# Gated mix of a complex state-space recurrence and a long convolution: convolution by a 32 x 64 transform in 64-row tiles with x kept in SBUF, recurrence over 8 time phases in stacks of 64 states, output in three column parts

## The chip, the cores and the metric

The kernel runs on one core of a Trainium2 chip. A core has a matrix engine (TensorE; PE in the profile, with its weight loads shown apart as PEld), a vector engine (DVE), a scalar engine (ACT), a general engine (POOL) and a queue engine (SP). TensorE reads from the on-chip memory SBUF (128 partitions) and writes to the accumulators in PSUM (8 banks of 512 fp32 words per partition); the other engines carry results from PSUM back to SBUF. DMA moves data between device memory and SBUF. The metric is the device time of one execution in microseconds; lower is better.

## The reference, cut to what matters

S = 2048 time steps, D = 1024 channels, P = 1024 complex states, all inputs in bf16. `_A_ref` is a linear recurrence with complex states, `_B_ref` a causal convolution of length 2048 per channel, and a gate mixes the two.

```python
def _A_ref(x, Lambda_re, Lambda_im, B_re, B_im, C_re, C_im, log_dt, Dskip):
    ...
    Lam_bar = jnp.exp(dt * Lam)
    B_bar = ((Lam_bar - 1.0) / Lam)[:, None] * Bmat
    Bu = jnp.einsum("bld,pd->blp", x + 0j, B_bar)
    ...
    for t in range(L):
        h = Lam_bar[None, :] * h + Bu[:, t, :]
        hs.append(h)
    ...
    y = 2.0 * jnp.einsum("blp,dp->bld", hseq, Cmat).real + x * Dskip[None, None, :]

def _B_ref(q, k, v, shift_k, ssm_k, ssm_D):
    ...
    for t in range(ks):
        k_shift = k_shift + k_pad[:, t:t + S, :] * shift_k[:, ks - 1 - t][None, None, :]
    kv = k_shift * v
    ...
    y = y + kv * ssm_D[None, None, :]
    return q * y

x = A_x
g = _sigmoid((x * gate_w).sum(-1, keepdims=True))
a = _A_ref(x, A_Lambda_re, A_Lambda_im, A_B_re, A_B_im, A_C_re, A_C_im, A_log_dt, A_Dskip)
b = _B_ref(x, B_k, B_v, B_shift_k, B_ssm_k, B_ssm_D)
return g * a + (1 - g) * b
```

Between the two lines on kv, `_B_ref` computes the causal convolution of kv with ssm_k by transforms of twice the length.

## The kernel before, in words

The work is written as a list of operations (`op`, and `dma` for transfers), each with an engine, a planned duration, the tiles it reads and writes, and a due time (the tables `PS`, `PU`, `PO`, `PC`, `PH`, `PG`). A planner, `_Plan.schedule`, runs through them in planned time, gives each a place in one of 21 slabs of SBUF or in PSUM, and so fixes the order on every engine; some operations may go to a second engine (`alt`), as evacuations from PSUM do (`evac`, line 520: ACT, or else DVE). `emit` then writes the instructions in that order. At run time an engine takes its instructions in order and waits by semaphores.

Recurrence (`s5`). x arrives by transposing DMA as four tiles `xT`, even and odd times in two halves of 512. For each of 8 groups of 128 states, `gemm_u` (line 882) multiplies x by the group's B, real and imaginary part apart, 512 columns a time; for even times the previous odd time's part comes in through the small diagonal matrices `dg` (lines 889, 892). `rot` turns the even times by a table of angles, scans them over time with a real factor (line 923) and turns them back (line 911 and the adds behind it); `odd` (lines 948, 950) makes the odd times from the even ones. Four of the 8 groups go to device memory (`h_scr`) and are read again for the output.

Convolution (`conv`), in 8 units of 128 channels. `kvprep` makes kv (lines 724 to 739) with channels on partitions and writes it to `kv_scr`; `load_A` reads it, and ssm_k, with 8 channels times 16 time blocks on partitions. `stage1` (line 747) takes the transform of length 16, `spec` (lines 760 to 762) the one of length 128, `product` (lines 772, 776) multiplies the two spectra on DVE, `inverse` (lines 786 to 788) goes back by the length 128, a DMA from slab to slab brings the 16 blocks onto partitions (line 515, four for each quarter), and `final` (lines 805 to 808) ends the transform, multiplies by x, read once more, and writes the result to `pB_scr`.

Output (`outp`). For each of 2 halves of the columns and 16 blocks of 128 rows, 16 matmuls of 512 columns (line 1125) sum h times C over the states; x (line 1099, times Dskip) and the convolution's result (line 1107, times 1 - g) come from device memory and are added (lines 1113, 1134). C is loaded by transposing DMA and scaled on ACT and DVE (lines 1053 to 1065).

At the start, 24 small matmuls (line 397) and the function `keep` (lines 1002 to 1014, several tile shapes) fill the time before x arrives; `gates` (line 964) computes the gate with weights of 32 columns.

The matmul of the transform in `gemm_u` reads

```python
PE_.matmul(ps.ap[:, ri, k0:k1], lhsT=BT.ap[:, d, ri, :], rhs=t.ap[:, d, k0:k1],
```

and that of the first step of the convolution, in `stage1`,

```python
PE_.matmul(ps.ap[:, i, :], lhsT=a.ap[:, 8 * q + i, :], rhs=t1v[:, hh * 128:(hh + 1) * 128],
```

## Time and profile before

| what | before |
|---|---|
| median of 3 runs | 431.93 us (429.65 to 432.07) |
| span of the profiled execution, first to last instruction | 427.0 us |
| median less span | 4.9 us |
| TensorE busy, granted clock | 398.4 us, 0.990 |
| VectorE, ScalarE, GpSimd busy | 346.7, 267.8, 132.7 us |
| DMA | 71.87 MB, 168 GB/s over the span |
| instructions | 7194, of them 2691 matmuls |

The profile is one execution. Busy time is the time in which an engine has an instruction running; matmuls are pipelined, so a matmul's mean duration is longer than its distance from the next, and the busy time of a dense run of matmuls counts each moment once. A group's line gives the source line, the engine, the operation, out<-in, shapes and count, then busy time, mean ns of one, and the idle time just before them with what ended it. For a matmul, 128*64 is the size of the stationary operand: rows (the contraction) by columns; 128x256 is the moving operand.

### The profile page before, as it was taken

To read this page: it belongs to the slowest core of one execution; us is meant where nothing else is said; L and a number is where in the kernel's file an instruction comes from. 1 tells how busy PE (TensorE), PEld (TensorE's weight loads), DVE (VectorE), ACT (ScalarE), POOL (GpSimd) and SP (SyncE) were. 2 spreads that over 40 slices of the span, in tenths; PEclk is the share of its full clock that TensorE was granted. 3 is DMA by queue.
4 is the path that set the end of the run, shared out by engine and by line. 5 is a ranking of instruction groups with operands and counts; after the bars stand their busy time and mean duration, and the time that the engine had idled before them with its cause. 6 is when DMAs were issued, how large, how long until landed. Compare 5 with 4: busy or idle time off the path is not lost.

```text
span 427.0 us, 7194 instructions
## 1 busy us (share of the span) xinstructions
PE 398.4 (93%) x2691; PEld 228.5 (54%) x2736; DVE 346.7 (81%) x513; ACT 267.8 (63%) x310; POOL 132.7 (31%) x172
## 2 busy tenths in 40 slices
PE   7598999999999789999969999899989999999996
PEld 6353544655566456566635655676544444444442
DVE  4998999999979789989889989979696969724422
ACT  3489488747589679477966786999554286203100
POOL 6994611232464134753634403340010000000000
PEclk9999999999999999999998999999999999999999
DMA  8999999459999999598999369999989996405111
GB/s 149 113 196 195 194 232 231 174 90 160 158 186 193 256 217 185 127 207 173 187 184 164 90 192 166 287 184 178 174 163 185 213 234 205 143 22 177 49 37 62
DMA packets 153596, 71.87 MB, mean 168 GB/s; under 512 B 129861, under 2 KB 147541, under 8 KB 153561
## 3 DMA queue, kind: packets, MB, share of 16 engines
q1 hardware_dynamic: 146120, 54.55, 69.8%
q0 software_dynamic: 7360, 16.85, 16.9%
q8 instruction: 21, 0.34, 0.4%
q14 instruction: 15, 0.11, 0.1%
q10 hardware_dynamic: 80, 0.01, 0.0%
HBM read 24.93 MB, written 16.79 MB: 98 GB/s over the span
## 4 chain that ended last, share of the span: by engine, by line
PE 68%; DMA 11%; SPq 10%; ACT 4%; DVE 3%; issue 3%; POOL 0%; DVEq 0%; ACTq 0%; POOLq 0%
PE ps L1125 22%; PE ps L882 20%; SPq L513 8%; DMA slab<-slab 5%; PE ps L760 4%; ACT slab L520 4%; PE ps L747 4%; DMA slab<-in_A_x_dram 4%; PE ps L889 3%; PE ps L950 3%; DMA slab<-in_B_ssm_k_dram 3%; PE ps L761 2%; PE ps L786 2%; PE ps L762 2%; SPq L515 2%
## 5 line engine op out<-in xcount | busy, mean ns | idle before, releaser
L520 ACT CAST slab<-ps 128x1024 bf16<-128x1024 f32 x197 | 185.4, 1042 | 62.8 <-PE ps L892 17.6
L882 PE MATMUL ps<-slab,slab 128*128 128x512 bf16 (+1 forms) x527 | 115.8, 370 | 6.3 <-DMA slab<-in_A_B_re_dram 3.1
L1125 PE MATMUL ps<-slab,slab 128*128 128x512 bf16 x485 | 109.1, 379 | 1.0 <-DVE slab L1134 0.4
L882 PEld LDWEIGHTS <-slab 128*128 128x128 bf16 x544 | 52.8, 99 | 60.0 <-issue 5.5
L1125 PEld LDWEIGHTS <-slab 128*128 128x128 bf16 x512 | 49.8, 98 | 59.6 <-issue 0.7
L515 POOL DMA_DIRECT2D slab<-slab x84 | 51.4, 618 | 57.8 <-ACT slab L520 51.9
L1134 DVE SCALAR_TENSOR_TENSOR slab<-ps,gcols,slab 128x512 bf16<-128x512 f32 x32 | 23.6, 747 | 39.1 <-PE ps L1125 36.1
L1107 ACT ACTIVATE slab<-slab,omgc 128x512 bf16<-128x512 bf16 x32 | 21.2, 714 | 45.2 <-DMA slab<-pB_scr 40.1
L760 PE MATMUL ps<-slab,fC 128*128 128x512 bf16 x118 | 44.9, 381 | 1.1 <-ACT slab L520 0.6
L747 PE MATMUL ps<-tab,slab 128*128 128x128 bf16 x512 | 35.0, 222 | 7.5 <-POOL slab L712 6.2
L911 DVE TENSOR_TENSOR slab<-slab,slab 128x2048 bf16<-128x2048 bf16 x31 | 37.7, 1217 | 3.5 <-PE ps L747 1.5
L772 DVE TENSOR_TENSOR slab<-slab 128x2048 bf16<-128x2048 bf16 x32 | 38.6, 1215 | 1.8 <-ACT slab L520 1.5
L747 PEld LDWEIGHTS <-slab 128*128 128x128 bf16 x512 | 31.4, 99 | 12.3 <-POOL slab L712 6.8
L761 PE MATMUL ps<-slab,fS 128*128 128x256 bf16 x128 | 35.0, 273 | 0.6 <-issue 0.2
L762 PE MATMUL ps<-slab,fN 128*128 128x256 bf16 x128 | 35.0, 274 | 0.0
L786 PE MATMUL ps<-slab,gC 128*128 128x256 bf16 x128 | 29.9, 273 | 1.7 <-DVE slab L776 1.7
L776 DVE TENSOR_TENSOR slab<-slab 128x512 bf16<-128x512 bf16 x64 | 24.9, 416 | 6.3 <-PE ps L950 2.3
L788 PE MATMUL ps<-slab,gS 128*128 128x128 bf16 x128 | 28.0, 219 | 0.0
L787 PE MATMUL ps<-slab,gN 128*128 128x128 bf16 x128 | 28.0, 219 | 0.0
L735 DVE TENSOR_TENSOR slab<-slab,slab 128x2047 bf16<-128x2047 bf16 (+2 forms) x22 | 26.7, 1213 | 0.0
L808 DVE TENSOR_TENSOR slab<-ps,slab 128x1024 bf16<-128x1024 f32 x16 | 19.3, 1216 | 3.3 <-PE ps L806 2.8
L1113 DVE SCALAR_TENSOR_TENSOR slab<-slab,gcols,slab 128x512 bf16<-128x512 bf16 x26 | 18.3, 745 | 3.5 <-ACT slab L1107 3.4
(184 smaller groups left out, 532.5 us busy)
## 6 DMA issues: line engine op xcount, KB each, us to landing
slab<-in_A_x_dram SPq DMA_DIRECT2D x22, 256.0 KB
slab<-slab POOLq DMA_DIRECT2D x84, 64.0 KB, 5.3
slab<-h_scr SPq DMA_DIRECT2D x8, 512.0 KB
slab<-pB_scr SPq DMA_DIRECT2D x16, 256.0 KB
out_dram<-slab SPq DMA_DIRECT2D x15, 256.0 KB
slab<-in_B_ssm_k_dram SPq DMA_DIRECT2D x7, 512.0 KB
pB_scr<-slab SPq DMA_DIRECT2D x12, 256.0 KB
slab<-slab SPq DMA_DIRECT2D x44, 64.0 KB
```

Of the source, the lines that this page charges most:

```text
L513: nc.sync.dma_start_transpose(out=o_, in_=i_)
L515: QS[q].dma_start(out=o_, in_=i_)
L520: op("ACT", 1.04, lambda: A.copy(o_(), i_()), r=r, w=w, prio=prio, alt=("DVE", 1.2, lambda: V.tensor_copy(o_(), i_())))
L747: PE_.matmul(ps.ap[:, i, :], lhsT=a.ap[:, 8 * q + i, :], rhs=t1v[:, hh * 128:(hh + 1) * 128], start=True, stop=True)
L760: PE_.matmul(ps.ap[:, i], lhsT=fC[:, k2, :], rhs=zz, start=True, stop=False)
L761: PE_.matmul(ps.ap[:, i, :, 0, :], lhsT=fS[:, k2, :], rhs=zz[:, :, 1, :], start=False, stop=False)
L762: PE_.matmul(ps.ap[:, i, :, 1, :], lhsT=fN[:, k2, :], rhs=zz[:, :, 0, :], start=False, stop=True)
L772: TT(out=T.ap, in0=K.unsqueeze(2).to_broadcast([128, 2, 2, 4 * CH]), in1=W_.unsqueeze(1).to_broadcast([128, 2, 2, 4 * CH]), op=ALU.mult)
L786: PE_.matmul(ps.ap[:, i], lhsT=gC[:, k2, :], rhs=pp.ap[:, :, i, :], start=True, stop=False)
L882: PE_.matmul(ps.ap[:, ri, k0:k1], lhsT=BT.ap[:, d, ri, :], rhs=t.ap[:, d, k0:k1], start=(d == 0), stop=(par == 1 and d == ND - 1))
L911: TT(out=out, in0=tab.ap.unsqueeze(2).to_broadcast([128, 2, 2, CW]), in1=x.unsqueeze(1).to_broadcast([128, 2, 2, CW]), op=ALU.mult)
L1125: PE_.matmul(ps.ap, lhsT=Hr[pi, a // 4].ap[:, par, ri, (a % 4) * 128:(a % 4 + 1) * 128], rhs=CT[pi, dh][0].ap[:, CT[pi, dh][1], ri, :], st ...
```

## The change

The kernel is rewritten around the same planner (places are now in units of 1 KB of 9 slabs, due times in one table). What it does now:

- x stays in SBUF in natural layout as `X` (16 row groups of 128, 32 KB a partition); it is scaled by 1 - g there, multiplied by the convolution's result there, and added in the output. `pB_scr` and `kv_scr` are gone.
- The transform of the convolution is 32 times 64. `stage1` uses the data as the stationary operand, in four tiles of 64x64, and so has time on partitions at once; `spec` uses two tiles of 128x64; `inverse` two of 64x128, with two or four terms (`TERMS`: for four, the sums of the complex product are left to PSUM, and `product` leaves out its two adds). Where DMA brought blocks onto partitions, DVE transposes blocks of 32x32 (`turn` in `kvprep`, `flip`).
- The recurrence has 64 states, real and imaginary part stacked, on 128 partitions. Time is cut in 8 phases (t mod 8) of 256. `gemm` adds up four phases in a chain, in two halves (`hn`, `jn`), the scan runs over 256 (`turned`), and `fill` makes the other phases from it.
- All of h goes to device memory except that the last two groups are used from SBUF in part one. The output runs in three column parts (`PARTS`: 256, 512, 256 columns); each part reads h again, part three only the half that part two's tiles don't still hold (`SHARE`). The output's matmuls use two tiles of 128x64, and x times Dskip is a matmul for all rows.
- C isn't scaled any more (the factor is in the recurrence's small matrices); three DMAs swap halves of each C tile.

Core of the diff (removed lines only where they stand for a replaced function):

```diff
-    NSLAB, NPS = 21, 8
+    NSLAB, NPS = 9, 8
...
+TERMS = (2,2,2,4,4,4,4,4)
...
+PARTS = ((0,2),(2,4),(6,2))
+SHARE = {(2, ph): (1, ph) for ph in range(4, 8)}
...
+    X = consts.tile([128, 16, D], BF16, name="X")
...
-        def stage1(a, z, w, hh, q, pr):
+        def stage1(a, z, w, j, pr):
...
-                for i in range(8):
-                    PE_.matmul(ps.ap[:, i, :], lhsT=a.ap[:, 8 * q + i, :], rhs=t1v[:, hh * 128:(hh + 1) * 128],
-                               start=True, stop=True)
+                for i in range(8):
+                    for h in range(2):
+                        for r_ in range(2):
+                            PE_.matmul(ps.ap[64 * r_:64 * r_ + 64, h, i, :], lhsT=av_[64 * h:64 * h + 64, 8 * j + i, :],
+                                       rhs=t1[64 * h:64 * h + 64, r_].rearrange("p k b -> p (k b)"), start=True, stop=True)
+            evac(lambda: z.ap[:, :, w, :].rearrange("p k (h b c) -> p k h b c", h=2, b=2)[:, :, :, :, 8 * j:8 * j + 8],
+                 lambda: ps.ap.rearrange("p h c (k b) -> p k h b c", b=2), r=[ps], w=[(z, (w, j))], pr=pr)
...
-        def spec(z, kv, q, h, pr):
+        def spec(z, kv, q, hh, pr):
...
-                    PE_.matmul(ps.ap[:, i], lhsT=fC[:, k2, :], rhs=zz, start=True, stop=False)
-                    PE_.matmul(ps.ap[:, i, :, 0, :], lhsT=fS[:, k2, :], rhs=zz[:, :, 1, :], start=False, stop=False)
-                    PE_.matmul(ps.ap[:, i, :, 1, :], lhsT=fN[:, k2, :], rhs=zz[:, :, 0, :], start=False, stop=True)
+                    for r_ in range(2):
+                        for h in range(2):
+                            PE_.matmul(ps.ap[64 * h:64 * h + 64, i, r_], lhsT=Wt[:, k2, r_, :], rhs=z.ap[:, k2, :, 64 * h:64 * h + 64],
+                                       start=True, stop=True)
...
+            for i, o_ in enumerate((ALU.subtract, ALU.add)[:4 - nt]):
+                op("DVE", 0.43, lambda i=i, o_=o_: TT(out=T.ap[:, 0, i], in0=T.ap[:, 0, i], in1=T.ap[:, 1, 1 - i], op=o_), r=[T], w=[T], prio=pr)
...
+                for k in range(8):
+                    for i, (a, b, sl) in enumerate(terms):
+                        for h in range(2):
+                            hs = slice(64 * h, 64 * h + 64)
+                            PE_.matmul(ps.ap[:, h, :, k, :],
+                                       lhsT=Gt[hs, 8 * q + k].rearrange("p a b -> p (a b)")[:, 64 * (sl + NG - 4):64 * (sl + NG - 2)],
+                                       rhs=T.ap[hs, a, b, k, :].rearrange("p (a b) -> p a b", b=2), start=(i == 0), stop=(i == nt - 1))
...
-            dma("SP", 1.15, lambda: [zb.ap[4 * q + i:128:16].rearrange("s g r c -> s g (r c)") for i in range(4)],
-                lambda: [qq.ap[:, i].rearrange("p r c -> p (r c)") for i in range(4)], [qq], [(zb, q)], pr, n=4, issue=0.65, alt="POOL")
+        def flip(qt, qf, h, pr):
+            cs = slice(32 * h, 32 * h + 32)
+            op("DVE", 1.26, lambda: V.transpose(qf.ap.rearrange("p w g e -> p (w g e)").bitcast(F32),
+                                               qt.ap[:, cs].rearrange("p w k e -> p (w k e)").bitcast(F32)),
+               r=[qt], w=[qf], prio=pr)
...
+        def gemm(pi, b, BT, mt_, H):
+            ps = pl.psum([2, 2, M])
+
+            def f(a):
+                for s_ in range(2):
+                    for d in range(ND):
+                        PE_.matmul(ps.ap[:, a, s_, :], lhsT=BT.ap[:, d, s_].rearrange("p r c -> p (r c)"), rhs=xT[4 * a + b].ap[:, d, :],
+                                   start=(s_ == 0 and d == 0), stop=(b == 0 and s_ == 1 and d == ND - 1))
...
+                def hn():
+                    for a in range(2):
+                        for s_ in range(2):
+                            PE_.matmul(ps.ap[:, a, s_, :], lhsT=mt_[s_].ap[:, 6 - b % 2].rearrange("p b c -> p (b c)"), rhs=H[b - 1].ap[:, a, s_, :],
+                                       start=False, stop=(s_ == 1 and not (b == 3 and a == 1)))
...
+            dma("SP", ws, lambda: [w.ap[0:64]], [lambda: t.ap[0:64, :, 1, :]], [(t, 1)], [w], pr, alt="POOL")
+            dma("SP", ws, lambda: [t.ap[0:64, :, 1, :]], [lambda: t.ap[64:128, :, 0, :]], [(t, 0), w], [(t, 1)], pr, alt="POOL")
+            dma("SP", ws, lambda: [t.ap[64:128, :, 0, :]], [lambda: w.ap[0:64]], [w, (t, 1)], [(t, 0)], pr, alt="POOL")
...
+            for i0, i1 in ((0, 3), (3, 6)) if pt == 0 else ((0, 4), (4, 8)):
...
+        def outp(pt, ph):
...
+                        for s_ in range(2):
+                            for h in range(2):
+                                H_ = Ht.ap[:, i, s_] if i < ni else Hs[i][ph % 4].ap[:, ph // 4, s_]
+                                PE_.matmul(ps.ap[64 * h:64 * h + 64, :], lhsT=H_[:, 2 * h + xx:M:4], rhs=c_.ap[:, k, s_, :],
+                                           start=(i == 0 and s_ == 0), stop=(i == NP - 1 and s_ == 1))
+                        for db in range(nu) if i == 0 else ():
+                            for h in range(2):
+                                PE_.matmul(ps.ap[64 * h:64 * h + 64, db * 128:(db + 1) * 128], lhsT=xt.ap[:, db, 2 * h + xx:M:4],
+                                           rhs=dskd[:, u0 + db, :], start=False, stop=False)
```

## The prediction

> **What bounds the kernel now.** I read the busy line of the page first, then the chain that ended last, then the windows by stage, and last the time line of TensorE for prices.
>
> ```profile
> PE 398.4 (93%) x2691; PEld 228.5 (54%) x2736; DVE 346.7 (81%) x513; ACT 267.8 (63%) x310; POOL 132.7 (31%) x172
> DMA  8999999459999999598999369999989996405111
> PE 68%; DMA 11%; SPq 10%; ACT 4%; DVE 3%; issue 3%; POOL 0%; DVEq 0%; ACTq 0%; POOLq 0%
> ```
>
> TensorE is busy for 93% and carries 68% of the chain; VectorE is close behind (81%), and the DMA engines are nearly full until the last tenth. So the kernel is bound by TensorE with little slack elsewhere.
>
> ```profile
> 10.00:20.00 10.00, 4.80 (x40) 3.50 (x38) 9.67 (x20) 3.85 (x8) 9.08 (x7) 0.97 1.32 105
> 140.00:160.00 20.00, 16.44 (x118) 9.56 (x120) 16.16 (x25) 13.35 (x16) 5.33 (x8) 1.00 1.17 242
> 220.00:240.00 20.00, 16.75 (x121) 10.94 (x124) 17.99 (x29) 15.39 (x17) 7.62 (x11) 0.91 0.88 160
> 260.00:280.00 20.00, 18.70 (x165) 12.72 (x166) 19.48 (x27) 16.84 (x19) 8.31 (x11) 1.00 0.95 243
> 400.00:420.00 20.00, 19.90 (x93) 9.02 (x93) 4.92 (x8) 0.00 (x0) 0.00 (x0) 1.00 0.13 46
> ```
>
> Columns: stretch, length, busy time of PE, PEld, DVE, ACT, POOL, clock, DMA share, GB/s. TensorE loses time in the first 40 us (x and B arrive) and in a few dips; the output stage at the end is TensorE alone. DMA moves at most about 243 GB/s over 20 us.
>
> ```profile
> 8.44 0.75 PE L1010 MATMUL ps<-ident 64*64 64x128 bf16 x20
> 9.12 0.50 PE L1014 MATMUL ps<-ident 64*128 64x256 bf16 x6
> 9.55 0.62 PE L604 MATMUL ps<-dskd,ones 128*128 128x128 bf16 x8
> 10.01 1.91 PE L882 MATMUL ps<-slab,slab 128*128 128x256 bf16 x16
> 37.00 1.91 PE L964 MATMUL ps<-slab,gwb 128*32 128x512 bf16 x31 [0.88 <-DMA slab<-in_A_x_dram]
> ```
>
> These give prices, start to start. L882: 16 of 256 columns in 1.91 less the 0.27 of the last, over 15: 109 ns. L604, 128 columns: (0.62 - 0.22)/7 = 57 ns; 16 of L747 take 0.89, 55.6 ns each. 512 columns: 32 of L882 in 6.91, 216 ns. L964 uses a quarter of the array's columns: (1.91 - 0.38) over 30 is 51 ns for 512 columns, so four ran side by side. L1010 uses 64x64 tiles: (0.75 - 0.31) over 4 steps is 110 ns for four of 128 columns, in a stretch at half pace (the 24 of L397 just before take (2.74 - 0.31)/23 = 106 ns each for the same columns). So small tiles do run in parallel.
>
> **TensorE, before and after.** Before: 1248 matmuls of 512 columns at 0.216 are 269.6 (transform of x 512, recurrence 160, convolution's last step 64, output 512); first conv step 512 x 0.0556 = 28.5; spectra 128 x (0.216 + 2 x 0.109) = 55.6; inverse 128 x (0.109 + 2 x 0.0556) = 28.2; gate 1.7. Sum 383.6. The span is 427.0, so 43.4 us are not streamed: about 22 of them in the first 40 us, 4 at the tail, 17 in dips.
> After, from the order of its instructions: transform of x 1024 x 0.109 = 111.6; recurrence 400 x 0.109 = 43.6 (was 34.6: more block terms); spectra 1024 half-array matmuls in pairs of 128 columns, 512 x 0.0556 = 28.5 (was 55.6: the second transform is 64 long, not 128); last conv step 32 pairs x 0.216 = 6.9 (was 13.8); output 256 pairs of 256, 256 of 512 and 256 of 256 columns: 256 x 0.434 = 111.1 (same); the x times Dskip term on TensorE for all rows, 128 pairs x 0.0556 = 7.1 (was under 1); gate 1.7.
> Two terms have no exact row. First conv step: 2048 matmuls of 64x64 tiles, 64 columns. Low end: four at a time at half of 55.6, 512 x 27.8 = 14.2. High end: each alone, 2048 x 27.8 = 57. L1010 is the nearest row (same tiles, four together, starts spread over 9 ns), so I take 27.8 + 7 = 35 ns, 17.9. Inverse: 1664 matmuls of 64 rows and 64 columns in pairs; 23 to 46, taken as 832 x 31 ns = 25.8 (L1014's pairs start 3 ns apart).
> Sum 354.2. New: 141 changes of tile shape. Between L1014's last start (9.35, plus 0.107) and L604's (9.55) 0.10 us are lost, so 141 x 0.10 = 14.1; the low end is 0 (waits hide them). Total 368, against 383.6: 15 us less.
> The Trainium skill (TensorEngine Tiling, Instruction Overhead) says that each matmul has about 60 cycles of overhead and that a tiling factor should not be taken from a dimension that is already small; at 2.4 GHz that is 25 ns, the two small-tile steps would cost 3712 x 25 = 93 us and the time would be 460, an estimate from that page. The trace has four starts of 64x64 tiles within 9 ns, which speaks against it, but only 20 matmuls in a row.
>
> **VectorE and ScalarE.** Rows used:
>
> ```profile
> L520 ACT CAST slab<-ps 128x1024 bf16<-128x1024 f32 x197 | 185.4, 1042 | 62.8 <-PE ps L892 17.6
> L911 DVE TENSOR_TENSOR slab<-slab,slab 128x2048 bf16<-128x2048 bf16 x31 | 37.7, 1217 | 3.5 <-PE ps L747 1.5
> L772 DVE TENSOR_TENSOR slab<-slab 128x2048 bf16<-128x2048 bf16 x32 | 38.6, 1215 | 1.8 <-ACT slab L520 1.5
> L1134 DVE SCALAR_TENSOR_TENSOR slab<-ps,gcols,slab 128x512 bf16<-128x512 f32 x32 | 23.6, 747 | 39.1 <-PE ps L1125 36.1
> ```
>
> The four rows price most of it. Removed from VectorE: rotations 38.9, scans 38.2, their adds 27, scaling of C 18.5, x and gate products 31: 154 us. Kept: products 38.9, kv preparation 58, last conv product 16 x 1.216 = 19.5. Added: 24 block transposes of 1024 fp32 (no row; low 1.21 as the 1024-wide copy from PSUM, high 2.4 as two 512-wide scans; I take 1.5 = 36), half-width rotations 16 x 0.68 = 10.9, half scans 9.9, pair sums 24 x 0.416 = 10, matrices and tables 20, output 16 x 0.747 + 32 x 0.45 = 26, scaling of x 4, 48 full and 7 half evacuations 63, setup 30 (the 19 busy between 10 and 30 us now, and half as much again for the smaller operations). Sum 327, was 347. ScalarE: 160 x 1.042 + 24 x 0.57 = 180 of evacuations, 55 of tables and scaling: 236, was 268. The 64 evacuations of the first conv step read PSUM with a stride of 64 words, which no row has: at 1.04 nothing changes, at twice that 67 us are shared by two engines. I take 1.04. Up to the start of the output parts (some 200 us of TensorE work) the two engines have about 198 us of work each, so VectorE stays co-critical there, as it is now.
>
> **DMA.** 65 MiB (68 MB) against 71.87 MB: gone are the round trips of kv, of pB and of the inverse transform (24 MiB); h goes from 4 MiB written and 4 read to 8 and 18; three swaps per C tile are new (3 MiB). At the page's mean (86.7% of 427.0 for 71.87 MB, 5.15 us per MB) that is 351 us, was 370: the same density. K now comes in runs of 128 bytes, half of today's 256. For that 128-byte packet no row exists; if it costs as much as the 256-byte one, 4 MiB of K take twice their time, some 20 us of DMA time beside other work. Issue on SP grows from 57 to 104 transposes, mostly smaller; SP is on the chain only in the first 40 us, where x takes eight transposes as now. The three swaps of a C tile wait for one another; a slab-to-slab transfer takes 5.3 us from issue to landing, so a tile is ready 16 us after its load. I cost that at nothing, since the part before covers it; without that cover the first output matmul of a part waits up to 16, and on SP the x loads and output stores queued behind a waiting swap wait too.
>
> **Sum.** Not streamed: start and tail as now (26). The dips of 17 are partly waits for round trips that vanish (pieces of 7.7, 5.8 and 6.2 us for slab from slab in the chain), but VectorE and the four-step chain of evacuations per state block bring others: I take 12. Span 368 + 26 + 12 = 406. The median of the runs, 431.93, is 4.9 over the profiled span; with that, 411.
>
> **Rivals.**
> 1. The column parts wait for h. After the convolution, parts two and three move 12 MiB of h, 3 of x, 5.25 of C with its swaps and 3 of output: 24.4 MB, at 243 GB/s 100 us, for 89 us of TensorE work. If C of part two and four tiles of h (7.5 MiB, 32 us) come ahead, it fits; if less than a third of that does, or the rate falls to 225, 10 to 20 us are added: 421 to 431. For it: DMA is already at nine tenths. Against: shares of 1.17 occur, and part of the end is free now.
> 2. Slower: small-tile matmuls are bound by their issue, not by the array. 16,294 TensorE instructions against 5,474. At 27.8 ns each without overlap the two steps cost 103 instead of 44: 470. It turns slower than now where the two steps cost 44 + 21 = 65 us, 17.5 ns per small matmul instead of 11.8. The 256-column work between the bursts lets a queue refill, so half of it, 440, is likelier than all. For it: no stretch of the trace shows more than one matmul per 27 ns for long. Against: the starts of L1010.
> 3. Better: switches hide behind waits and the dips go: 354 + 26 + 8 + 5 = 393.
>
> **Numbers.** Forecast 0.48, rival 1 0.18, rival 2 0.22, rival 3 0.12. The likeliest time is 411; its own range 400 to 421. The range 392 to 445 takes in rivals 1 and 3 and the milder half of rival 2. A measurement of this kernel tells about 1% from no change (427.6 to 436.3): faster 0.70 (forecast, rival 3, and 0.10 of rival 1), within 0.09 (the rest of rival 1 and a little of 2), slower 0.21.
>
> **What would show it.** The 32 matmuls of one buffer of the first conv step start within 0.28 us if I am right, within 0.9 if rival 2 is. TensorE busy near 385; spectra group half of today's. VectorE near 327, the transposes 1.2 to 2.4 each. Idle before the output matmuls caused by DMA from h_scr means rival 1. Strided evacuations well above 1.04, or TensorE idle behind ScalarE before the output parts, would make the sum wrong at its dips.

## The result, and the profile after

The changed kernel takes 492.54 us (median of 4 runs, 491.71 to 495.51), the kernel before 432.0 in the same session (429.65 to 432.25): 1.143 times as long, 95% interval 1.136 to 1.150. The forecast was 411, its range 392 to 445: wrong, and on the wrong side. The profiled execution has a span of 490.2 us (before 427.0, the forecast's sum for the span 406). In the table below a median is that of all executions of a kernel and a ratio that of the executions within 1.5% of the fastest; one execution of e10_replan, 798.6 us with TensorE at half pace throughout, is left out.

The page of the changed kernel, the lines that answer to those shown of before, and two more (granted clock, instruction queue):

```profile
PE 409.9 (84%) x8146; PEld 337.6 (69%) x8146; DVE 321.8 (66%) x447; ACT 223.7 (46%) x243; POOL 97.5 (20%) x139
...
PE   6689559999879999998696984996795899998874
...
PEclk9999869999989999999597988899899999999998
DMA  4999985551775534299873989449859458873211
...
q8 instruction: 64, 1.05, 1.0%
...
PE 63%; DVE 10%; issue 8%; SPq 8%; DMA 5%; ACT 4%; DVEq 0%; ACTq 0%
```

VectorE and ScalarE have less to do than before, as planned, and are idle for a third (VectorE) and half (ScalarE) of the time. TensorE is still the longest, but its row has holes all along, and its clock is no longer full in many slices. "issue", time in which an engine waits for nothing that the profile shows, has gone from 3% to 8% of the chain. The queue q8, which brings instructions, has 64 packets where the page of before has `q8 instruction: 21, 0.34, 0.4%`.

The windows by stage, same columns as in the prediction:

```profile
60.00:80.00 20.00, 12.96 (x345) 9.90 (x333) 13.70 (x18) 13.90 (x18) 6.38 (x10) 0.74 0.86 180
180.00:200.00 20.00, 19.51 (x374) 15.47 (x372) 16.75 (x19) 13.89 (x17) 3.60 (x7) 1.00 0.41 95
300.00:320.00 20.00, 13.92 (x406) 12.60 (x404) 10.73 (x11) 10.72 (x10) 0.00 (x0) 0.91 0.66 84
460.00:480.00 20.00, 15.40 (x268) 13.81 (x266) 3.87 (x8) 0.00 (x0) 0.00 (x0) 1.00 0.15 35
```

From 300 to 320 us TensorE is idle for 6 of 20 us while VectorE and ScalarE are idle for 9 each and DMA is at two thirds: nothing in these columns is the limit. In the last stage, where TensorE alone had work and was busy for 19.90 of 20 before, it now is for 15.40.

What TensorE waited for, total us, times, longest:

```profile
PE ps L1094 <- issue: 15.8, 5, 5.1
PE ps L1094 <- DVE slab L1105: 11.1, 18, 1.7
PE ps L768 <- issue: 9.8, 5, 4.2
PE ps L809 <- issue: 7.6, 4, 2.6
PE ps L906 <- DVE slab L589: 5.2, 1, 5.2
```

There are two new kinds of idle time. One is "issue": 33 us in the first, third and fourth line. The other is a wait of the output matmuls (L1094) for VectorE's step that reads the accumulator (L1105), 18 times, though VectorE is nearly free at that time. Around 300 us, the time line of TensorE:

```profile
293.29 0.71 PE L768 MATMUL ps<-t,slab 64*64 64x64 bf16 x64
293.99 0.38 PE L1094 MATMUL ps<-slab,slab 128*64 128x256 bf16 x3
296.65 0.43 PE L1094 MATMUL ps<-slab,slab 128*64 128x256 bf16 x1 [2.28 <-issue]
...
299.36 0.58 PE L768 MATMUL ps<-t,slab 64*64 64x64 bf16 x32
299.87 1.11 PE L809 MATMUL ps<-slab,Gt 64*128 64x64 bf16 x64
300.91 0.44 PE L1094 MATMUL ps<-slab 128*64 128x256 bf16 x4
301.18 0.38 PE L1094 MATMUL ps<-slab,slab 128*64 128x256 bf16 x3
306.69 0.43 PE L1094 MATMUL ps<-slab,slab 128*64 128x256 bf16 x1 [5.13 <-issue]
```

The stops fall in the middle of an accumulation, between two matmuls of one line that wait for no semaphore. Bursts of the small-tile steps (L768, L809) come shortly ahead of them. Counting TensorE's records shows where: each of the 15 stops of over 0.3 us stands 256 instructions, or a multiple of 256, from the others, and ends 2.3 to 3.0 us after a packet of q8 starts. A packet is 16,384 bytes, so 64 bytes for each of 256 instructions; 64 packets carry the 16,294 instructions of TensorE. In the kernel before, two packets are never closer than 13.3 us; here the closest are 3.5 apart. Of the 59 blocks entered after 60 us (the entry is counted from the start of the last matmul of the block before), 39 have the packet of the next block started within 2 us of the entry; for the other 20 it starts 2 to 9.6 us after it (mean 5.0), and there the 16 DMA engines are 95% busy on average. In the first 2 us after the entry they are 94% busy for the late packets and 53% for the others. That gave the first theory (F): TensorE's instructions come in blocks of 256, about one block ahead, through the same DMA engines as the data; where a block's work is shorter than the way to the next block, TensorE stops, and its clock is often halved for a while (ten of the 15 stops lie in or just ahead of a stretch at half clock).

Three sums are used below for TensorE after the first 20 us: idle ahead of matmuls that wait for no semaphore (but for changes of tile shape), idle ahead of matmuls that wait for one (both with gaps down to 25 ns), and time at half clock. A gap is counted from the end of the array time of the matmul before, which lies some 0.17 us ahead of the end in its record, so it is longer by this than in a time line. Half clock is the length of the clock's records that start after 20 us.

| kernel | median us | ratio to before, 95% | span | no semaphore | semaphore | half clock |
|---|---|---|---|---|---|---|
| before | 432.0 | | 427.0 | 9.6 (0.4 in gaps over 0.3) | 20.0 | 7.0 |
| changed | 492.5 | 1.143 (1.136 to 1.150) | 490.2 | 38.4 (37.2) | 49.9 | 55.9 |
| e1_wide | 492.9 | 1.150 (1.135 to 1.166) | 490.8 | 35.3 | 55.5 | 61.7 |
| e2_bank | 487.9 | 1.138 (1.121 to 1.154) | 481.3 | 41.4 | 39.6 | 62.1 |
| e3_split128 | 434.8 | | 430.1 | 7.8 | 18.8 | 12.7 |
| e4_split64 | 451.3 | 1.056 (1.043 to 1.068) | 446.2 | 14.3 | 21.0 | 15.2 |
| e5_half | 472.5 | 1.097 (1.085 to 1.109) | 474.7 | 22.9 | 56.8 | 41.1 |
| e6_light | 471.4 | 1.095 (1.083 to 1.106) | 466.9 | 17.0 | 50.0 | 44.7 |
| e7_start | 493.0 | 1.146 (1.134 to 1.158) | 482.6 | 40.9 | 44.1 | 60.8 |
| e8_three | 444.1 | 1.027 (1.010 to 1.043) | 442.7 | 4.8 | 50.4 | 28.6 |
| e11_xlater | 446.7 | 1.044 (1.025 to 1.062) | 446.4 | 6.4 | 57.0 | 28.9 |
| e12_xgate | 440.3 | 1.032 (1.025 to 1.039) | 436.9 | 6.3 | 44.0 | 18.2 |
| e13_fix | 494.2 | 1.157 (1.147 to 1.168) | 488.7 | 40.9 | 43.7 | 60.6 |
| e14_again (= e10_replan) | 505.5, one run | | 503.7 | 32.2 | 73.9 | 80.6 |

Spans are of single executions, and repeated runs of one kernel differ by 1 to 3%, so a difference of span of a few us is read only together with the gaps that explain it.

### The profile page after: what moved, and what is told of

It reads as the page before. It is cut to its first block, busy times and chain, and to the rows that moved or that the text cites. A ratio compares the mean times of both kernels' runs of the same rounds, so it can differ in the third digit from the quotient of the medians.

```text
span 490.2 us, 17861 instructions
## 1 busy us (share of the span) xinstructions
PE 409.9 (84%) x8146; PEld 337.6 (69%) x8146; DVE 321.8 (66%) x447; ACT 223.7 (46%) x243; POOL 97.5 (20%) x139
## 2 busy tenths in 40 slices
DMA packets 133252, 69.37 MB, mean 142 GB/s; under 512 B 113360, under 2 KB 125540, under 8 KB 132664
## 4 chain that ended last, share of the span: by engine, by line
PE 63%; DVE 10%; issue 8%; SPq 8%; DMA 5%; ACT 4%; DVEq 0%; ACTq 0%
PE ps L1094 24%; PE ps L906 15%; SPq L507 8%; PE ps L809 6%; PE ps L782 4%; ACT slab L515 3%; DVE slab L1105 3%; DMA slab<-in_B_v_dram 3%; PE ps L768 2%; PE ps L969 2%; DMA slab<-in_A_B_im_dram 2%; DVE slab L515 2%; PE ps L914 2%; PE ps L1098 1%; PE ps L975 1%
## 5 line engine op out<-in xcount | busy, mean ns | idle before, releaser
L515 ACT CAST slab<-ps 128x1024 bf16<-128x1024 f32 (+1 forms) x185 | 167.7, 965 | 183.8 <-PE ps L768 45.4
L1094 PE MATMUL ps<-slab,slab 128*64 128x256 bf16 (+1 forms) x1424 | 125.9, 317 | 26.7 <-issue 15.8
L1094 PEld LDWEIGHTS <-slab 128*64 128x64 bf16 x1536 | 95.7, 139 | 48.8 <-issue 34.4
L906 PE MATMUL ps<-slab,slab 128*128 128x256 bf16 x1024 | 120.2, 276 | 5.6 <-DVE slab L589 5.2
L906 PEld LDWEIGHTS <-slab 128*128 128x128 bf16 x1024 | 100.4, 99 | 20.2 <-issue 6.7
L1105 DVE SCALAR_TENSOR_TENSOR slab<-ps,gcols,X 128x256 bf16<-128x256 f32 (+1 forms) x48 | 26.9, 569 | 88.1 <-PE ps L1094 75.6
L515 DVE CAST slab<-ps 128x1024 bf16<-128x1024 f32 (+1 forms) x55 | 62.8, 1151 | 29.0 <-PE ps L768 9.2
L768 PE MATMUL ps<-t,slab 64*64 64x64 bf16 x2048 | 26.6, 200 | 16.0 <-issue 9.8
L809 PE MATMUL ps<-slab,Gt 64*128 64x64 bf16 x1664 | 31.9, 194 | 8.2 <-issue 7.6
L809 PEld LDWEIGHTS <-Gt 64*128 64x128 bf16 x1664 | 27.9, 97 | 15.6 <-issue 14.2
L768 PEld LDWEIGHTS <-slab 64*64 64x64 bf16 x2048 | 22.1, 112 | 23.7 <-issue 21.5
L782 PE MATMUL ps<-slab,Wt 128*64 128x128 bf16 x1024 | 36.2, 223 | 2.3 <-DVE slab L1105 1.3
L782 PEld LDWEIGHTS <-Wt 128*64 128x64 bf16 x1024 | 31.9, 112 | 6.8 <-issue 5.5
L509 POOL DMA_DIRECT2D h_scr<-slab x27 | 15.2, 563 | 97.1 <-ACT slab L515 80.1
L748 DVE TENSOR_TENSOR slab<-slab,slab 128x2045 bf16<-128x2045 bf16 (+2 forms) x21 | 25.6, 1219 | 0.7 <-ACT slab L746 0.4
L969 PE MATMUL ps<-slab,slab 128*128 128x256 bf16 x81 | 22.4, 305 | 0.7 <-ACT slab L515 0.4
L818 DVE STREAM_TRANSPOSE slab<-slab 128x1024 f32<-128x1024 f32 x16 | 19.0, 1221 | 4.9 <-ACT slab L515 4.8
```

Source lines behind the costliest of these rows:

```text
L509: QS[q].dma_start(out=o_, in_=i_)
L515: op("ACT", a, lambda: A.copy(o_(), i_()), r=r, w=w, prio=pr, alt=("DVE", d, lambda: V.tensor_copy(o_(), i_())))
L748: op("DVE", 1.23, lambda tmp=tmp, j=j, n=n: TT(out=acc.ap[:, j:S], in0=acc.ap[:, j:S], in1=tmp.ap[:, 0:n], op=ALU.add), r=[acc, tmp], w=[a ...
L768: PE_.matmul(ps.ap[64 * r_:64 * r_ + 64, h, i, :], lhsT=av_[64 * h:64 * h + 64, 8 * j + i, :], rhs=t1[64 * h:64 * h + 64, r_].rearrange("p ...
L782: PE_.matmul(ps.ap[64 * h:64 * h + 64, i, r_], lhsT=Wt[:, k2, r_, :], rhs=z.ap[:, k2, :, 64 * h:64 * h + 64], start=True, stop=True)
L809: PE_.matmul(ps.ap[:, h, :, k, :], lhsT=Gt[hs, 8 * q + k].rearrange("p a b -> p (a b)")[:, 64 * (sl + NG - 4):64 * (sl + NG - 2)], rhs=T.a ...
```

## The experiments

**First set: which instructions, and which wait.** Two changes to the new kernel, and two to the kernel before that only raise its number of instructions.

e1_wide, the output with one 128-column stationary tile in place of two of 64:

```diff
-                            for h in range(2):
...
-                                PE_.matmul(ps.ap[64 * h:64 * h + 64, :], lhsT=H_[:, 2 * h + xx:M:4], rhs=c_.ap[:, k, s_, :],
+                            PE_.matmul(ps.ap, lhsT=H_[:, xx:M:2], rhs=c_.ap[:, k, s_, :],
```

> The changed kernel with the output's matmuls as one 128-column stationary tile instead of two of 64 (every second row, not every fourth, so the rows of the output come out in another order within a block; the work is the same size). Array time is unchanged, TensorE has 1792 instructions fewer (14,502). Theory F (TensorE runs dry at every 256th instruction, because the next 16 KB of instructions come too late): the gaps without a semaphore in the output parts (18 us in the profile, at 290, 297, 307, 336, 350 and 378 us) all but vanish and with them some four half-clock windows of 3.4 us; 57 fetches instead of 64; 20 to 28 us faster, 464 to 472. Theory D (the output parts wait for h, x or C by DMA): nothing of that changes, 489 to 493.

Measured: 492.9. Theory F in this form fell: 1,792 fewer instructions in the output parts gained nothing. The idle without a semaphore stayed (35.3 us), but all of it now stands in the three small-tile steps of the convolution. So the number of instructions as such is not the loss; the bursts are. The time is the one that theory D had (489 to 493), but D's cause is not seen: in the changed kernel no wait of the output matmuls for h, x or C is in the list of waits, and e6_light below, which leaves out most of the reloads of h, has as much semaphore wait.

e2_bank, the last 16 accumulators of the output spread over the four PSUM tiles:

```diff
...
+    for k, t in enumerate(last[-16:]):
+        t.place = 2 * (k % 4)
```

> The changed kernel with the 16 output accumulators of part three spread over the four PSUM tiles in turn, not over the two halves of one; the order of the work is the same. Theory B (a matmul into one half of a PSUM tile waits until VectorE has read the other half): the 16 waits of 0.74 us in part three vanish, 11 to 13 us faster, 479 to 482. Rival: the waits are for the data, and nothing changes, 490 to 493.

Measured: span 481.3, 8.9 below, with 10.3 us less in semaphore waits. In the changed kernel, part three of the output looks so, in the time line of TensorE:

```profile
456.11 1.70 PE L1094 MATMUL ps<-slab,slab 128*64 128x256 bf16 x27
458.39 0.44 PE L1094 MATMUL ps<-slab,slab 128*64 128x256 bf16 x4 [0.58 <-DVE slab L1105]
```

and in e2_bank so:

```profile
456.39 1.97 PE L1094 MATMUL ps<-slab,slab 128*64 128x256 bf16 x32
458.14 0.33 PE L1098 MATMUL ps<-dskd,slab 128*64 128x128 bf16 x4
458.26 1.97 PE L1094 MATMUL ps<-slab,slab 128*64 128x256 bf16 x32
```

An accumulator every 2.67 us became one every 1.87. An accumulator of one bank shares a PSUM tile with another, and the next accumulation waited, by semaphore, until VectorE had read the other half; before, every accumulator took a whole tile. Theory B (the pairs) holds for this stretch: 16 times 0.80 us. In the whole time the gain is smaller and near the noise: the median is 4.6 us below that of the changed kernel, and the intervals of the two ratios overlap.

e3_split128 and e4_split64 cut the output matmuls of the kernel before from 512 columns into pieces of 128 and of 64 (8,546 and 12,642 instructions instead of 5,474), e4 so:

```diff
+                            for w0 in range(0, 512, 64):
+                                PE_.matmul(ps.ap[:, w0:w0 + 64],
...
```

> The kernel of before with each 512-column matmul of the output stage split into four of 128 columns with the same weights: the same array time but for 0.0556 x 4 against 0.216 us, 3072 more TensorE instructions, in a stretch with little DMA. 256 instructions last 7.1 us there. Theory F (a fetch takes some 2.5 us and is asked for about 100 instructions ahead, here 2.8 us): 0 to 6 us slower, 432 to 438. Theory I (each instruction costs TensorE time of its own): the same, since 27.8 ns per instruction is above its floor.

> As before, split into eight of 64 columns: 7168 more instructions, 128 pairs in about 3.6 to 3.8 us. Theory F: at every 256th instruction a gap of 1.0 to 1.5 us without a semaphore, some 32 of them, so 32 to 48 us on top of 0 to 12 for pairs of 30 ns instead of 27.8: 464 to 492. Theory I alone (28 to 30 ns a pair, evenly): 432 to 445, with no gaps at multiples of 256.

Measured: e3 434.8, no stop at a block's end, as both theories had it. e4 451.3, between the two theories: matmuls 29.2 ns apart, so 256 instructions in 3.7 us, packets of q8 3.3 to 4.4 us apart, and 4.9 us in five stops over 0.3 us instead of one in each block. At 14.6 ns per instruction the supply just keeps up in this stretch, where little else is loaded. The first conv step of the changed kernel uses a block in 128 x 8.8 ns = 1.1 us.

**Second set: bursts, transfers, start.** The theory, sharper: bursts use up the block ahead, and the next one comes later the busier the DMA engines are.

e5_half halves the matmuls of the two burst steps and leaves their array time; of the edit, the first step:

```diff
-                    for h in range(2):
-                        for r_ in range(2):
-                            PE_.matmul(ps.ap[64 * r_:64 * r_ + 64, h, i, :], lhsT=av_[64 * h:64 * h + 64, 8 * j + i, :],
-                                       rhs=t1[64 * h:64 * h + 64, r_].rearrange("p k b -> p (k b)"), start=True, stop=True)
+                    for h in range(2):
+                        PE_.matmul(ps.ap[c_:c_ + 64, h, n_:n_ + 2, :], lhsT=av_[64 * h:64 * h + 64, 8 * j + i, :],
+                                   rhs=t1[64 * h:64 * h + 64].rearrange("p r k b -> p r (k b)"), start=True, stop=True)
...
```

> The changed kernel with half as many matmuls in two steps and the same array time. First conv step: one 64-row tile moves both halves of the table at once (128 columns instead of 64), the column tiles taken by turns over the blocks; inverse: one matmul moves two neighbouring columns of k (128 moving columns instead of 64) by the first one's stationary tile. What is computed is so no longer right in these two steps (real and imaginary parts of the first step stand in other rows, every second column of the inverse uses its neighbour's matrix); loads, evacuations, VectorE work and the order of everything are the same. TensorE then has about 12,600 instructions instead of 16,294. Theory F (TensorE's instructions come in blocks of 256 through queue q8, and a block whose work is shorter than the way to the next block leaves TensorE without instructions): idle without a semaphore falls from 38 us to 5 to 18, half clock from 56 to under 35, span 490 to 435-460. Rival W (waits for other engines and for loads set the end, the gaps only stand where a wait would stand anyway): semaphore waits grow by what the gaps lose, span 480-492.

Measured: span 474.7; idle without a semaphore 22.9, half clock 41.1. Both fell, by less than F said, and 7 of the 15.5 us that the stops gave back went into semaphore waits; the span lies between F's range and W's. F's direction holds, rival W has a part.

e6_light moves less data with the same instructions (it leaves out a part of k, v and the reloads of h):

```diff
-                dma("SP", 0.425 * (i1 - i0), lambda i0=i0, i1=i1: [t.ap[:, i0:i1]],
+                dma("SP", 0.425 * (i1 - i0), lambda i0=i0, i1=i1: [t.ap[:, i0:i0 + 1]],
...
+            n0 = S if u < 2 else 512
```

> The changed kernel with less data moved and every instruction of TensorE, VectorE and ScalarE as it was: of each reload of h from DRAM only the first of its three or four groups is loaded (one quarter to one third of the bytes), and of k and v of units 2 to 7 only 512 of 2048 rows; the rest of these tiles holds what lay there before, so the output is wrong. Theory F with contention (a block of 256 instructions is asked for when the block before it is entered, and starts within 1 us where the DMA engines have room, but 3 to 9.6 us later where they are full, as the trace of the changed kernel has it): idle without a semaphore falls from 38 us to under 15 after 200 us into the span, where the loads are left out, the packets of q8 start within 2 us of the entry of a block there, half clock under 35 us, span 440-465. Rival (a fixed supply of 256 instructions per 3.4 to 4 us whatever else the DMA engines do): the idle stays above 25 us, span 475-490.

Measured: span 466.9; idle without a semaphore 17.0, of which 12 after 200 us; the packets of q8 there start at most 4.4 us after the entry of a block (9.6 in the changed kernel). Not one instruction less, and half of the stops' time is gone: a fixed supply is ruled out, the DMA load is part of it. Semaphore waits stay at 50.0, so what was gained is not the wait for the data left out. F's figures for the packets (within 2 us), for half clock (under 35 us) and, by 2 us, for the span were missed.

e7_start takes the first two x phases ahead of the second group's B:

```diff
...
+    for o in lead + first:
+        order.remove(o)
+    order[at:at] = lead + first
```

> The kernel e2_bank with one move on SP: the two transposes of B for the first group and those of x for the first two time phases go ahead of the B transposes of the second group (5.2 us of SP). The result stays right. Theory S (the start is late by what B's doubled transposes take on SP): the first transform matmul starts at 11 to 12 us instead of 16.7, and the span is 3 to 6 us below e2_bank's 481.3, that is 475-478. Rival (TensorE only waits for x later, or for VectorE's tables): span 480-482.

Measured: the first transform matmul starts at 12.5 us instead of 16.8, and the span is 482.6, as e2_bank's 481.3. Theory S fell: TensorE then waits for the later x phases and, 2.1 us twice, for the small matrices from GpSimd and VectorE (L877), which are no earlier. The late start is there, and costs nothing of its own.

**Third set: the supply by itself, and the sum.** e9_rate adds 1,024 small matmuls behind the last output, and 1,024 more beside ten loads of 1 MB:

```diff
+        for n in range(1024):
+            h, r_, t = 64 * (n // 2 % 2), 64 * (n % 2), slabs[3 + n // 4 % 5]
+            PE_.matmul(psums[3][r_:r_ + 64, ...], lhsT=t[h:h + 64, 0:64], rhs=t[h:h + 64, 64:128], start=True, stop=True)
+        for n in range(10):
+            (nc.sync, nc.gpsimd)[n % 2].dma_start(out=..., in_=h_scr[n % 4]...)
+        for n in range(1024):
...
```

> The changed kernel, and behind its last output two more stretches that change nothing of it: 1,024 matmuls of 64x64 tiles with 64 columns, four tiles side by side, while nothing is loaded; then 1,024 more while ten loads of 1 MB from DRAM run. The result stays right. Each stretch has 2,048 TensorE instructions, eight blocks of 256. Theory F: the first stretch goes at the pace of the supply, 3.4 to 3.9 us for each block, 27 to 31 us; the second, with the DMA engines full, 5 to 9 us for each block while the loads last, 40 to 65 us. Theory A (the array alone sets the pace, 8.8 ns for one of four tiles side by side): 9 to 10 us for each stretch. A fixed supply that loads do not touch: 27 to 31 us for both.

The time line of TensorE, L1133 the quiet stretch, L1140 the one with loads:

```profile
504.53 1.27 PE L1133 MATMUL ps<-slab 64*64 64x64 bf16 x128 [2.56 <-issue]
508.27 1.92 PE L1133 MATMUL ps<-slab 64*64 64x64 bf16 x128 [2.48 <-issue]
512.29 1.92 PE L1133 MATMUL ps<-slab 64*64 64x64 bf16 x128 [2.10 <-issue]
...
533.49 1.92 PE L1140 MATMUL ps<-ident 64*64 64x64 bf16 x128 [4.57 <-issue]
540.52 1.92 PE L1140 MATMUL ps<-ident 64*64 64x64 bf16 x128 [5.11 <-issue]
547.28 1.92 PE L1140 MATMUL ps<-ident 64*64 64x64 bf16 x128 [4.84 <-issue]
...
563.73 1.92 PE L1140 MATMUL ps<-ident 64*64 64x64 bf16 x128 [1.55 <-issue]
```

This is the plainest line of the study: 128 matmuls, that is 256 instructions, a stop, 128 matmuls, a stop. Quiet, a block comes every 3.78 us (500.51 to 527.00, seven blocks), whether its work takes 1.27 or 1.92; with the DMA engines full (share 1.04), every 6.69 us (533.49 to 560.25, four blocks); when the loads end, 3.5 to 4.0 again. The quiet stretch took 28.3 us, the loaded one 44.5, both where theory F had them; the array alone would need 9 to 10 at full clock and twice that at half. The mean granted clock is 0.61 from 500 to 526 us and 0.50 from 528 to 558.

e8_three puts e5_half, e6_light and e2_bank together:

> The edits of e5_half, e6_light and e2_bank together: half as many matmuls in the first conv step and the inverse at the same array time (both steps no longer right), a part of the bytes of k, v and the reloads of h left out (so the output is wrong), and the last 16 output accumulators each in a PSUM tile of its own. Theory F (blocks of 256 instructions, late where the DMA engines are full) and theory B (waits between the halves of one PSUM tile) as the two main causes of the loss: idle without a semaphore under 8 us, half clock under 30 us, span 430-448, near the kernel before (427). Rival W (what is gained there is lost again to waits for other engines and for loads): semaphore waits above 55 us and span 455 or more.

```profile
PE 393.5 (89%) x6290; PEld 326.6 (74%) x6290; DVE 321.4 (73%) x447; ACT 223.2 (50%) x243; POOL 88.6 (20%) x139
```

Measured: span 442.7. The three gains alone are 8.9, 15.5 and 23.3, in sum 47.7; together they are 47.5. Idle without a semaphore is 4.8, the clock 0.969. By medians they are 4.6, 20.0 and 21.1, and 48.5 together. Supply (with the data that make it late) and PSUM pairs are shown as the cause of 47.5 of the 84 us between forecast and measurement. But semaphore waits are still 50.4 us, and with all three edits, two of which leave work out, it is not faster than the kernel before.

**Fourth set: the waits that stay.** In e8_three TensorE is busy for 26.83 us between 40 and 80 us (39.57 before). Its VectorE there:

```profile
52.92 0.75 DVE L739 TENSOR_SCALAR slab<-slab,skc 128x2048 bf16<-128x2048 bf16 x1 [8.75 <-DMA slab<-in_B_k_dram]
...
73.28 0.69 DVE L932 TENSOR_TENSOR slab<-slab,slab 128x1024 bf16<-128x1024 bf16 x1 [6.07 <-DMA g_scr<-slab]
```

k of unit 0 comes late, and behind it stand on VectorE the steps that the recurrence needs. At 30 us GpSimd had issued five loads of 512 KB, x in natural layout, which the change keeps in SBUF. e11_xlater moves them behind the first addition to ssm_k:

```diff
...
+    for o in late:
+        order.remove(o)
+    at = order.index(add) + 1
+    order[at:at] = late
```

> The kernel e8_three (span 442.7, the same parts left out) with one move on GpSimd's queue: five of the six loads of x in natural layout (512 KB each), issued at 30 us in e8_three, go behind the first addition to ssm_k. In e8_three VectorE waits 8.75 us for k of unit 0 at 44 us and 6.07 us more at 67 us behind SP, whose transpose of v takes 17.15 us, and TensorE waits 4.5 and 5.3 us for VectorE there. Theory X (the loads of x that is now kept in SBUF hold back k and v in the full DMA engines, and VectorE, then TensorE, wait for them): these waits go, VectorE's wait for k falls below 3 us, span 430-437. Rival (the early stage is bound elsewhere, or x comes too late for its scaling then): span 440-446.

Measured: 446.4, no gain. The wait for k is gone, and a longer one has come:

```profile
77.36 0.69 DVE L932 TENSOR_TENSOR slab<-slab,slab 128x1024 bf16<-128x1024 bf16 x1 [18.73 <-DMA g_scr<-slab]
```

The store of the gate's row is queued on SP behind the landing of the next B transposes, 25.6 us, which now share the DMA engines with the loads of x. e12_xgate and e13_fix, e12 in e8_three and e13 in e2_bank, move all eight loads of x behind the gate:

```diff
+    late = sorted((o for o in order if o.dma == 1.7), key=lambda o: o.idx)[:8]
...
+    at = order.index(gate) + 1
+    order[at:at] = [o for o in late if o.eng == "POOL"]
```

> The kernel e8_three (span 442.7, the same parts left out) with all eight loads of x in natural layout (4 MB in all) moved behind the gate: six on GpSimd's queue behind the loads of the gate's columns, two on SP behind the store of the gate's row. In e11_xlater, where they went only behind the first addition to ssm_k, VectorE no longer waited for k, but 18.7 us for a slab that the store of the gate's row still read; that store stood on SP behind the landing of two transposes of B, for 25.6 us. Theory X2 (whatever is loaded while these 4 MB are in the queues comes 10 to 25 us late, and the wait only moved): now neither k nor B is late, TensorE's busy time between 40 and 80 us rises from 26.8 to 35 or more, semaphore waits fall from 50 to 35-40, span 428-436. Rival (the wait moves on once more, to x itself, whose scaling began at 105 us, or to the conv's first units): span 440-448.

> The changed kernel with the two repairs that leave the result right and all work in place: the last 16 output accumulators each in a PSUM tile of its own (e2_bank, span 481.3) and the loads of x in natural layout behind the gate (as e12_xgate). Theory X2: 8 to 13 us below e2_bank, span 468-474; idle without a semaphore stays at 35-45 us. Rival (moved wait): span 478-485.

Measured: e12 436.9, TensorE busy for 34.39 us between 40 and 80, semaphore waits 44.0. All three miss what was expected, busy time and span by less than 1 us, and the span lies between the theory's range and the rival's. Against the kernel before, run beside each, nothing is gained: 1.032 times as long, and 1.027 for e8_three. At 97.5 us TensorE waits 3.5 us for the next B. e13 488.7 is outside both ranges, and worse than e2_bank's 481.3 if anything (1.157 times the kernel before, against 1.138): there the wait for B at 107 us is 7.24. So in the three places tried for these 4 MB, the transposes queued with them come late, and the wait moves. No version with all its work in place came near the kernel before.

e10_replan gives the same operations another order and other places, worked out with the supply in the planner:

> The changed kernel with the same operations in another order: the order and the places come from the same planner, but it now counts TensorE's instructions (after each 256 it waits for the next block, which it takes to come 3 us after the block before was entered, later by 0.45 of the transfers then in hand, 5.4 us at most), plans 1.31 us for a 64-row transpose on SP, and gives every accumulator a PSUM tile of its own; 300,000 trials of due times. It plans 449 us for this order and 490 for the due times of the changed kernel, of which 34 and 59 us are waits for instructions. The result stays right. Theory F (supply, PSUM pairs): span 440-465, idle without a semaphore 15-30 us, half clock below 45 us. Rival W (the time is set by the waits for other engines in whatever order): span 475-495.

> The kernel e10_replan once more, for a profile of an undisturbed execution (its profiled one took 798 us with TensorE at half pace throughout, the other three 488 to 509). If theory F's planner model holds and only its other durations are off: idle without a semaphore 15-30 us and semaphore waits above 60. If the model of the supply is what fails: idle without a semaphore 35 us or more, as in the changed kernel.

Measured: 488.5, 490.9 and 508.5 in three runs of e10_replan, and a profile of 503.7 in e14_again. The planned 34 us of waits for instructions were 32.2, just above the 15 to 30 expected, so the model of the supply was about right; but it saved only 6 us of stops and nothing of the time, which lies where rival W had it or above. The semaphore waits, 73.9 us, show where the loss is now: from 20 to 40 us TensorE is busy for 5.83 us, since five transposes of x that took 13 us on SP now take 40.49. The plan had put other loads beside them, which its model of the DMA engines let pass.

## Why the prediction was wrong

- **Prices of the small-tile steps.** Right. Inside a buffer at full clock the first conv step takes 8.8 ns for a matmul (35 ns for four, as taken; 0.27 us for 32), the inverse 29 ns for a pair (31 taken), spectra 55, transform 109. The sign named for rival 2 (0.9 us for 32) did not show. The 141 changes of shape, taken at 14.1 us, were right too: 29 stand where there is no semaphore and cost 2.8 us, 0.095 each, and the 112 others have a median gap of 0.098 us, 95 of them under 0.2. By this some 11 of the 49.9 us of the semaphore column are changes of shape.
- **The other engines.** Right: VectorE 321.8 us (327), ScalarE 223.7 (236), 69.37 MB (68). The lines that had no row before, in the costliest groups by form:

```profile
L818 DVE STREAM_TRANSPOSE slab<-slab 128x1024 f32<-128x1024 f32 x16 | 19.0, 1221 | 4.9 <-ACT slab L515 4.8
L753 DVE STREAM_TRANSPOSE slab<-slab 128x1024 f32<-128x1024 f32 x8 | 16.7, 2092 | 0.1
L515 ACT CAST slab<-ps 128x1024 bf16<-128x1024 f32 x160 | 155.9, 1023 | 160.7 <-PE ps L768 45.4 <-PE ps L809 44.9 <-PE ps L782 37.3
```

  24 transposes took 35.7 us (36 taken), the strided evacuations are no dearer.
- **The step that failed** is the one from array time to elapsed time, "Not streamed: ... I take 12" for the dips and the verdict on rival 2. Both assumed that TensorE's instructions are there when the array is free. Rival 2 had the right count (16,294 instead of 5,474) and the wrong price: a matmul that waits for its own issue. The 20 matmuls of L1010 refuted that price rightly, but said nothing of 256. The measured price is by the block: 3.8 us for each 256 instructions in a quiet stretch (packets were never closer than 3.3), 6.7 with the DMA engines full, for work of 1.1 us in the first conv step. In the changed kernel that made 15 stops, 37.2 us, for which the sum had no term. Its sign stood in the page of before, the 21 packets of q8, and was not read.
- **The price of a small matmul and of a block.** The Trainium skill's rule that the prediction weighed (TensorEngine Tiling (Array Packing), Instruction Overhead) gave 460 and the measurement lies beyond that, but not by its mechanism: 8.8 ns between small matmuls is below its 25. A page that bears on the loss was not drawn on: the Trainium skill (Runtime: NRT & Kernel Launch, Instruction fetch mechanics) says that instructions come in 16 KiB blocks of 256, the next while the current one runs, and that the cost is mostly hidden. The trace agrees on the block and not on "hidden": 38.4 us.
- **The clock.** TensorE is at half clock for 55.9 us (7.0 before), in stretches of 3.4, 6.8 and 10.2 us; by an estimate from these two figures, up to half of the difference, 24 us, is time lost, and the sum had no term for it. The Trainium skill (TensorE: Matmul & The Clock Gate, Part 1) says that the clock is halved after an idle window of about 3.4 us. The trace agrees on the length, and less than a whole idle window was enough: counted in pieces of 3.41 us, after the first 20 us, the array had work for 0 to 36% of the eleven pieces after which the clock went to half, and for at least 41% of those after which it stayed full. It came back to full after pieces with at least 80%. This fits e9_rate, which stays at half: a block there has work for at most 1.92 of 3.78 us.
- **Dips.** Taken at 12 us of waits, measured 49.9 in the semaphore column, some 39 without the changes of shape. 10.3 are the PSUM pairs (e2_bank), a step that the prediction did not see: accumulators of up to 512 columns now take one bank. In e8_three TensorE is busy for 12.7 us less between 40 and 80 us than before; with the loads of x moved, 7.6 of these came back (e12_xgate), but not in the whole time. That the other 5 go to the same cause is not shown. The rest, many waits of 0.2 to 2 us for evacuations and VectorE, was not taken apart and stays open.
- **SP at the start.** "x takes eight transposes as now" was right of x and missed B: eight transposes of 64 rows, 1.31 us each, as much as one of 128 rows before, come ahead of x. TensorE starts 6.8 us later; by e7_start that alone costs nothing. The reading that SP is on the chain only in the first 40 us was not quite right either: the chain of before has SP at 209, 287 and 320 us too, 6.0 us in all.
- **Rival 1** did not come: no wait of the output matmuls for the reloads of h, or for C, is in the list of waits, so C's swaps, costed at nothing, show no wait of their own. But the reloads were not free: with k and v they are a part of what makes the blocks late (e6_light).

## What to carry to other kernels

Before splitting matmuls into small tiles, divide the engine's instructions by 256 and compare the work in each block with the time that a block takes to come (here 3.8 us, 6.7 beside full DMA engines): the average had room here (64 blocks in 490 us), the bursts did not. Spread such bursts among long matmuls (the one other order tried here, e10_replan, took only 6 us off the stops), or keep the transfers thin beside them. In this program an accumulator that shares its PSUM tile with another also shares its waits, and a block of loads that may come late in itself still delayed the loads queued with it, in each place tried.

## What the runs showed of the hardware that was not expected

- A stop of TensorE at each 256th instruction, 1.6 to 2.6 us with a quiet DMA (0.57 at the first) and 4.3 to 5.1 beside ten loads of 1 MB (e9_rate), with about one block in hand.
- Four 64x64 tiles side by side at 8.8 ns a matmul, while the supply sustains one instruction in 14.8 ns (3.78 us for 256, e9_rate).
- A DMA transpose of 64 rows takes SP 1.31 us, one of 128 rows 1.35; with the DMA engines full, one transpose of v kept SP for 17.15 us in e8_three.
- The clock at half after pieces of 3.41 us in which the array had work for up to 36%, in the changed kernel, and not only after idle ones.
- A block transpose of 1024 fp32 on VectorE takes 1.22 us in one layout (L818) and 2.09 in another (L753).
